# Summing the first chunks' softmax weights by a column of ones behind the values, in an attention that feeds a gated product of matrices

## The chip, the cores and the metric

The kernel runs on one core of one Trainium2 chip. The metric is device time in microseconds. Three timed runs of the kernel before gave 703.55, 704.68 and 706.06 us; the median is 704.68. Besides there is one profiled execution, whose trace all the durations come from.

## What is computed

An attention over 4 batches, 8 heads, 768 positions and 64 features gives rows x (3072 tokens of 512 features), and these go through three weight matrices. Cut to what matters:

```python
k_sum = k.reshape(B, H, nb, 32, D).max(axis=3)
v_sum = v.reshape(B, H, nb, 32, D).mean(axis=3)
scores_l = scale * q @ k.T                     # kept where |i - j| < 16
scores_s = scale * (q @ k_sum.T) + log(32)
a = exp(concat(scores_l, scores_s) - max)
a = a / (sum(a) + 1e-9)
x = a @ concat(v, v_sum)
out = (x @ w_a) * (x @ w_b) @ w_out            # 512 to 1536, and back to 512
```

Each query thus sees the keys less than 16 positions away and 24 summaries of blocks of 32 positions: the largest of the keys, the mean of the values. The weights come as 64-bit floats.

## The kernel before

**Chunks and items.** The 3072 tokens are 12 chunks u of 256 tokens, each of two groups t of 128. The 1536 columns between the matrices are 12 slices f. One item is a chunk and a slice: the *up* makes x times the slice of w_a and of w_b, 24 matmuls at L932; ACT copies one product (L949), DVE multiplies by the other (L952), ACT rounds (L954), DVE makes the rest (L957); the *down* at L968 multiplies by the slice of w_out, four matmuls with the rounded part (gh) and two with the rest (gl). PE needs 2.75 us for an up at full clock and about 1.37 for a down. x and the weights are each split into a high and a low part, and three of the four products are made. Chunk 0's first two slices come first, then chunk 1 and chunk 0 in turn, then chunk after chunk.

**Weights.** The 36 parts (a, b, o of slice 0, then of slice 1, and so on) come in 18 pairs. A pair's two halves are converted from the raw 64-bit words: ACT scales the high words into bank c0 (L289), DVE makes three steps (L297, L304, L310), ACT rounds to the high part (L342), POOL subtracts and adds (L347, L353) to get the low one.

**First attention (chunks 0 and 1, four groups).** A group's queries are turned by PE (L374) and copied to qT by ACT (L806). PE puts the mask into two PSUM banks (L571), adds the dots with kT (L583), DVE takes the maxima (L616), ACT makes the exponentials (L628), and each of these is followed by a read of the sum that it gathered, which goes back into the bank. DVE adds 1e-9 and takes the reciprocal (L637, L643) and spreads it on a diagonal (L650); PE multiplies s by this diagonal, which turns it and normalises it (L671); ACT copies (L683); PE multiplies with the values (L712), which gives x with features on the partitions; ACT makes its high part (L720), DVE its low (L723). Groups 0 and 2 use banks o0 and o1, s and pt; groups 1 and 3 use o2 and o3 and space lent by weights that come later.

**Keys and means.** Six key tiles are turned by PE; ACT copies a tile's first part into kT (L433), DVE takes the blocks' largest (L443), ACT copies its other part (L435); when all six are done, POOL writes the summaries behind the keys (L409). Six pieces of v are summed by matmuls with a matrix of 1/32 (L825, two for each piece, one for each of the two rows that lie side by side on a partition); ACT copies the means behind the values (L837), POOL copies them for the other group (L843).

**Third chunk (u = 2).** It is done by DVE transposes instead: DVE adds the mask (L608) and takes maxima, ACT makes exponentials, POOL multiplies by the reciprocal (L658), DVE turns s into pt by twelve transposes of 32 rows (L698), PE multiplies with the values into bank c0. Both its groups use pt and c0, so the second group's transposes stand behind the first group's values.

**What sets the order.** Every operation is put into a list with an engine, a rank, a time it is thought to take, and the names that it reads and writes. A planner (Work, ahead of the kernel) then walks a clock: each engine takes, of the operations whose inputs it thinks ready, the one with the lowest rank. CHAIN is 0, FIRST (chunk 0) 1, CONVERT 2, NEXT (chunk 1) 2.3, SOON (third chunk) 5. The engines then run their queues strictly in that order, and SP issues the transfers in its own.

Of the kernel before, what the change touches and what calls it, by code (L numbers as in the profile page):

```python
# [9 lines left out]
F32 = mybir.dt.float32  # L10
# [4 lines left out]
AF = mybir.ActivationFunctionType  # L15
# [69 lines left out]
def attention_moe(  # L85
# [23 lines left out]
    NU = NR * B  # L109
    G = CH // P  # L110
    CV = 512
    NW = 3 * NF // 2
    AHEAD = (7, 9, 17)
# [81 lines left out]
    for j in (*range(8, 13), *range(NW - 3, NW)):  # L195
        spaces[f"W{j}"] = wp.tile([P, 2048], F32, tag=f"W{j}", name=f"space{j}")

    kins = [kin, spaces["S1"][:, 2 * CV : 2 * CV + S + 32]]
# [30 lines left out]
    CHAIN, FIRST, CONVERT, NEXT, SOON, PREP, LATER = 0, 1, 2, 2.3, 5, 5.5, 6  # L229
# [34 lines left out]
    slots = [("S0", 0), ("S0", 2), ("S1", 2)]  # L264

    def convert(j):
        rank = CONVERT + j / 4
# [58 lines left out]
        for hs in spans:  # L326
# [13 lines left out]
            act(  # L340
                rank - 0.5, 0.25 + 0.37 * len(hs), f + rk, hi,
                lambda ms=ms, f8=f8: nc.scalar.copy(out=parted(0)[:, ms], in_=f8),  # L342
            )
# [73 lines left out]
    def first_keys():  # L417
        n = P // BLK
        for i in range(S // P):
# [7 lines left out]
            pe(FIRST, 0.85, [key], [bk], lambda bk=bk, x=x: turn(bank[bk], x))  # L427
            c0 = PER * i

            def put(lo, bk=bk, c0=c0):  # L430
                tr = bank[bk].rearrange("p (c x) -> p c x", x=P)
                if lo:
                    nc.scalar.copy(out=kT[:, :, c0 + 16 : c0 + WIN], in_=tr[:, :, : WIN - 16])  # L433
                else:
                    nc.scalar.copy(  # L435
                        out=kT[:, :, c0 + P : c0 + PER + 16], in_=tr[:, :, WIN - 16 :]
                    )
# [11 lines left out]
        for c in range(NP):  # L449
            work.add("-", 0, 0, 0, [f"ksi{i}" for i in range(6)], [f"ks{c}"], lambda: None)  # L450
            reads = [f"kT{x}{i}" for i in range(6) for x in "lh"]
            work.add("-", 0, 0, 0, reads, [f"kT{c}k"], lambda: None)
# [94 lines left out]
    def load_values(b, t, vw, keys, rank):  # L547
# [3 lines left out]
        for i, (e, r0, lo, hi) in enumerate((  # L551
# [5 lines left out]
                rank, 2.1 * (hi - lo), 215, (), [keys[i]], vw[e][r0 : r0 + hi - lo],  # L557
# [3 lines left out]
    def scores(u, t, qT, qk, s, sk, banks, diag=None, lead=None):  # L561
        kind = 0 if t == 0 else 2 if t == S // P - 1 else 1
        rank = rank_of(u) + (0.2 * (t % G) if u < FILL else 0)
        m, mk = nml[t % 2], f"nml{t % 2}"


        masked = u < FILL

        def masks():
            for h in range(2):  # L570
# [476 lines left out]
```

## Time and profile before

| | us |
|---|---|
| median of three runs | 704.68 |
| profiled execution | 704.12 |
| its span | 702.4 |
| PE busy | 682.8 |
| first up begins | 37.08 |
| third chunk's first two ups begin | 160.90 |

The span is the time from the first to the last instruction in the trace; the execution's own time is 1.7 us longer. Mean granted clock of PE: 0.998. Rows of a timeline give the start, the time, the engine, the line, the operation with its output and input, the count, and in brackets the time without work before it with the engine and line that ended it. SPq is the queue that issues transfers; there the time is that of issuing.

### The profile page before, as it was taken

Reading aid. Unit: us, or ns where it says so; the run is one execution under the profiler, and the core shown is the slowest. Engines: PE = TensorE matmul, PEld = TensorE weight load, DVE = VectorE, ACT = ScalarE, POOL = GpSimd, SP = SyncE. Lnnn points to the kernel's source line nnn. Section 1 sums busy time; section 2 is a strip of 40 time slices with the busy share of each in tenths; the row PEclk is TensorE's granted clock in tenths of the full one; section 3 lists DMA queues with packets and bytes.
Section 4 is the critical chain, followed back from the end, with each engine's and each line's share of the span. In section 5 each row is a group of like instructions: output and inputs, shape, how many; then the busy total and the mean of one; then the engine's idle time right before and its main releaser. Section 6 shows DMA issues by size and latency. Waiting matters only on the chain.

```text
span 702.4 us, 15093 instructions
## 1 busy us (share of the span) xinstructions
PE 682.8 (97%) x6000; PEld 626.4 (89%) x6000; DVE 436.4 (62%) x988; ACT 252.4 (36%) x795; POOL 181.3 (26%) x219
## 2 busy tenths in 40 slices
PE   6888999999999999999999999999999999999997
PEld 3778999988999999999999999999999999999996
DVE  2898999797767777666763776762762662311221
ACT  2976574533333314332332323332331431211211
POOL 4378976852433521130110101110110110000000
PEclk9999999999999999999999999999999999999999
DMA  9979773076233335220300330310310100000000
GB/s 229 265 173 309 267 168 126 6 152 145 64 89 96 83 79 107 50 56 19 82 8 17 69 68 2 87 25 1 83 24 1 54 21 1 31 1 1 31 1 31
DMA packets 154943, 54.84 MB, mean 78 GB/s; under 512 B 132456, under 2 KB 147816, under 8 KB 154872
## 3 DMA queue, kind: packets, MB, share of 16 engines
q1 hardware_dynamic: 154872, 53.88, 31.5%
q8 instruction: 47, 0.77, 0.5%
q14 instruction: 24, 0.20, 0.1%
HBM read 47.12 MB, written 6.29 MB: 76 GB/s over the span
## 4 chain that ended last, share of the span: by engine, by line
PE 79%; DVE 7%; POOL 7%; issue 3%; ACT 2%; DMA 2%; SPq 0%; POOLq 0%; ACTq 0%; DVEq 0%
PE h L932 48%; PE o L968 24%; POOL w L353 3%; POOL S L347 2%; DVE c L304 2%; PE o L712 1%; PE c L712 1%; PE o L583 1%; PE c L583 1%; DVE space L297 1%; POOL space L347 1%; DVE space L310 1%; DMA raw<-in_moe_w_b_dram 1%; ACT s L628 1%; DVE ksum L443 1%
## 5 line engine op out<-in xcount | busy, mean ns | idle before, releaser
L932 PEld LDWEIGHTS h<-x,w 128*128 128x128 f32 x3456 | 416.0, 189 | 14.0 <-DVE x L723 2.2
L932 PE MATMUL h<-x,w 128*128 128x256 f32 x3456 | 419.4, 278 | 1.9 <-DVE x L723 1.7
L952 DVE TENSOR_TENSOR h<-h,g 128x256 f32<-128x256 f32 x144 | 62.2, 432 | 164.9 <-ACT g L949 163.2
L968 PE MATMUL o<-w,gh 128*128 128x512 f32 x576 | 157.8, 396 | 1.3 <-ACT gh L954 1.2
L949 ACT COPY g<-h 128x256 f32<-128x256 f32 x144 | 53.8, 374 | 280.8 <-PE h L932 279.9
L968 PEld LDWEIGHTS o<-w,gh 128*128 128x128 f32 x576 | 98.8, 188 | 18.6 <-ACT gh L954 2.3
L698 DVE STREAM_TRANSPOSE pt<-s 32x256 f32<-32x256 f32 x240 | 104.6, 436 | 8.7 <-POOL s L658 4.5
L658 POOL TENSOR_TENSOR s<-s,nml 128x512 f32<-128x512 f32 x40 | 41.6, 1042 | 257.0 <-DVE nml L643 255.5
L968 PE MATMUL o<-w,gl 128*128 128x512 f32 x288 | 90.1, 394 | 0.0
L957 DVE TENSOR_TENSOR gl<-h,gh 128x256 fp32r<-128x256 f32 x144 | 60.7, 422 | 31.6 <-ACT gh L954 30.2
L628 ACT ACTIVATE s<-s,nml 128x128 f32<-128x128 f32 x160 | 62.7, 398 | 43.3 <-DVE nml L616 43.3
L954 ACT CAST gh<-h 128x256 fp32r<-128x256 f32 x144 | 53.6, 372 | 67.6 <-DVE h L952 67.3
L968 PEld LDWEIGHTS o<-w,gl 128*128 128x128 f32 x288 | 53.8, 188 | 11.9 <-issue 0.3
L513 POOL TENSOR_TENSOR S<-S 96x512 f32<-96x512 f32 (+3 forms) x48 | 33.6, 699 | 39.1 <-DMA S<-in_v_dram 30.7
L347 POOL TENSOR_TENSOR space<-space,w 128x1024 f32<-128x1024 f32 (+1 forms) x13 | 26.7, 2056 | 18.8 <-ACT w L342 13.9
L628 ACT ACTIVATION_READ_ACCUMULATOR s<-s,nml 128x1 f32 x160 | 31.1, 194 | 0.0
L289 ACT ACTIVATE c<-raw 128x512 f32<-128x512 f32 x36 | 23.2, 644 | 13.2 <-DVE S L297 5.1
L353 POOL TENSOR_TENSOR w<-space 128x1024 fp32r<-128x1024 f32 (+1 forms) x13 | 26.8, 2059 | 0.9
L637 DVE TENSOR_SCALAR nml<-nml 128x4 f32<-128x4 f32 x40 | 9.8, 244 | 26.9 <-ACT s L628 26.9
L616 DVE TENSOR_REDUCE nml<-s 128x4 f32<-128x512 f32 x40 | 25.4, 669 | 0.0
L409 POOL COPY kT<-ksum 128x144 f32<-128x144 f32 x16 | 4.7, 308 | 61.5 <-DVE ksum L491 54.7
L347 POOL TENSOR_TENSOR S<-S,w 128x512 f32<-128x512 f32 (+1 forms) x11 | 17.6, 1598 | 9.7 <-ACT w L342 9.6
(100 smaller groups left out, 454.2 us busy)
## 6 DMA issues: line engine op xcount, KB each, us to landing
raw<-in_moe_w_a_dram SPq DMA_DIRECT2D x12, 512.0 KB
raw<-in_moe_w_b_dram SPq DMA_DIRECT2D x12, 512.0 KB
raw<-in_moe_w_out_dram SPq DMA_DIRECT2D x12, 512.0 KB
out_dram<-S SPq DMA_DIRECT2D x24, 256.0 KB
qin<-in_q_dram SPq DMA_DIRECT2D x160, 32.0 KB
S<-in_v_dram SPq DMA_DIRECT2D x24, 192.0 KB
vw<-in_v_dram SPq DMA_DIRECT2D x18, 192.0 KB
kin<-in_k_dram SPq DMA_DIRECT2D x24, 100.0 KB
```

Of the source, the lines that this page charges most:

```text
L347: lambda ms=ms, f8=f8: nc.gpsimd.tensor_tensor(out=f8, in0=f8, in1=parted(0)[:, ms].bitcast(F32), op=ALU.subtract),
L353: lambda ms=ms, f8=f8, p8=p8: nc.gpsimd.tensor_tensor(out=parted(1)[:, ms], in0=f8, in1=p8, op=ALU.add),
L513: lambda: nc.gpsimd.tensor_tensor(out=out, in0=i0, in1=i1, op=ALU.add),
L628: lambda h=h, c=c, sums=sums: nc.scalar.activation(s[h][:, c, :], x[h][:, c, :], AF.Exp, bias=m[:, 0, h, c : c + 1], scale=1.0, accum_out= ...
L658: lambda h=h, r=r: nc.gpsimd.tensor_tensor(out=s[h], in0=s[h], in1=r[:, :, None].broadcast_to([P, NP, P]), op=ALU.mult,),
L698: lambda js=js, qs=qs: nc.vector.transpose(out=pv[js, :, qs], in_=sv[qs, :, js]),
L932: nc.tensor.matmul(ps, w[:, c, part, :], x[xpart][:, c, :], start=(i == 0), stop=(i == n - 1))
L949: act(CHAIN, 0.38, [hk], [gk], lambda: nc.scalar.copy(out=g, in_=pa))
L952: lambda: nc.vector.tensor_tensor(out=pa, in0=pb, in1=g, op=ALU.mult),
L954: act(CHAIN, 0.41, [hk], [ghk], lambda: nc.scalar.copy(out=gh, in_=pa))
L957: lambda: nc.vector.tensor_tensor(out=gl, in0=pa, in1=gh.bitcast(F32), op=ALU.subtract),
L968: nc.tensor.matmul(bank[ok[j]], (gh if first else gl)[:, js], w[:, :, part, :], start=(f == 0 and first and part == 0), stop=(f == NF - 1 ...
```

## The change

- **Sums by ones.** In the first attention the exponentials no longer gather sums. The values get a 65th column of ones (VP = 80 columns are set aside for a head), in W13 for groups 0 and 2 and in W12 and S1 for 1 and 3. s is turned as it is, by plain transposes. The values' matmul has the queries on the partitions and writes 65 columns for each of the eight heads, four heads in a bank; the 65th is the sum. Per bank DVE then adds 1e-9, takes the reciprocal and multiplies 256 columns; PE turns the 512 columns back (the function turn), and the split into high and low part follows.
- **Keys.** Both ACT copies of a key tile are one step, and DVE's reduction waits for it. The masks wait for the first key turn only.
- **POOL.** For the first four pairs the rounding to the high part goes from ACT to POOL. POOL adds the two rows of each v piece, and the matmuls for the means fall from twelve to six. POOL makes four copies of the means instead of two, and fills the ones.
- **Third chunk.** The second group's transposes get a place of their own (pown, in S0, cleared by POOL) and follow its scores; its values go to bank c1. The third chunk's loads of queries wait for the fifth pair's conversion.
- **Ranks.** NEXT goes from 2.3 to 1.5, the conversions' rank from 2 + j/4 to 2 + j/6, the loads of the first pair from 8 and 9 to 5 and 5.5; three slots that the conversions use in turn are renumbered.

The diff, cut to its core:

```diff
-    CHAIN, FIRST, CONVERT, NEXT, SOON, PREP, LATER = 0, 1, 2, 2.3, 5, 5.5, 6
+    CHAIN, FIRST, CONVERT, NEXT, SOON, PREP, LATER = 0, 1, 2, 1.5, 5, 5.5, 6
...
-            act(
-                rank - 0.5, 0.25 + 0.37 * len(hs), f + rk, hi,
-                lambda ms=ms, f8=f8: nc.scalar.copy(out=parted(0)[:, ms], in_=f8),
-            )
+            if j < FIRSTS:
+                pool(
+                    rank - 0.5, 0.1 + 0.55 * len(hs), f + rk, hi,
+                    lambda ms=ms, f8=f8: nc.gpsimd.tensor_copy(out=parted(0)[:, ms], in_=f8),
+                )
+            else:
+                act(
...
-            act(FIRST, 0.43, [bk], [f"kTl{i}"], lambda put=put: put(True))
-            act(FIRST, 0.33, [bk], [f"kTh{i}"], lambda put=put: put(False))
+            act(FIRST, 0.75, [bk], [f"kT{i}"], put)
             dve(
-                FIRST, 0.6, [bk], [f"ksi{i}"],
+                FIRST, 0.6, [bk, f"kT{i}"], [f"ksi{i}"],
...
+    def early_scores(u, t, qT, qk, s, sk, banks):
...
+                act(
+                    rank, 0.26, [f"{mk}m{h}", banks[h]], [sk[h]],
+                    lambda h=h, c=c: nc.scalar.activation(
+                        s[h][:, c, :], x[h][:, c, :], AF.Exp, bias=m[:, 0, h, c : c + 1]
+                    ),
+                )
+
+    def early_values(u, t, s, sk, banks, pt, vw, vk):
...
+        def turned(h):
+            for c in range(NP):
+                nc.tensor.transpose(bank[banks[h]][:, c * P : (c + 1) * P], s[h][:, c, :], ident)
...
+        def weigh(j):
+            for i in range(NP):
+                g = NP * j + i
+                for e in range(2):
+                    es = slice(e * QT, (e + 1) * QT)
+                    nc.tensor.matmul(
+                        ps[j][es, i, : D + 1], d[:, g % 2, g // 2, es], vw[e][:, g, : D + 1],
+                        start=True, stop=True, tile_position=(0, e * QT),
+                    )
...
+        for j in range(2):
+            l = m[:, 1, j, :]
+            dve(
+                rank, 0.15, [banks[j]], [f"{mk}l"],
+                lambda j=j, l=l: nc.vector.tensor_scalar(
+                    out=l, in0=ps[j][:, :, D], scalar1=1e-9, scalar2=None, op0=ALU.add
+                ),
+            )
+            dve(rank, 0.15, [], [f"{mk}l"], lambda l=l: nc.vector.reciprocal(out=l, in_=l))
+            dve(
+                rank, 0.4, [banks[j], f"{mk}l"], [sk[0]],
+                lambda j=j, l=l: nc.vector.tensor_tensor(
+                    out=xn[:, j * 256 : (j + 1) * 256].rearrange("p (g d) -> p g d", d=D),
+                    in0=ps[j][:, :, :D], in1=l[:, :, None].broadcast_to([P, NP, D]), op=ALU.mult,
+                ),
+            )
+        pe(-1, 0.6, [sk[0]], [banks[1]], lambda: turn(bank[banks[1]], xn))
+        split(u, t, banks[1])
...
+        for x in vw0 + vw1:
+            nc.gpsimd.memset(x[:, :, D : D + 1], 1.0)
...
         for n in range(6):
-            pe(FIRST + 0.5, 1.0, [vin[n][1], mk], ["h0"], lambda n=n: means(n))
+            x, key = vin[n]
+            pool(
+                FIRST, 0.7, [], [key],
+                lambda x=x: nc.gpsimd.tensor_tensor(
+                    out=x[:, :, :D], in0=x[:, :, :D], in1=x[:, :, D:], op=ALU.add
+                ),
+            )
+            pe(FIRST + 0.5, 0.5, [key, mk], ["h0"], lambda n=n: means(n))
...
-            qk += blocks(98, f"qin.{c}", qin[:, c, :], q, b, c, r * CH)
+            qk += blocks(
+                98, f"qin.{c}", qin[:, c, :], q, b, c, r * CH, ["done4"] if u == FILL else ()
+            )
...
             begin(1)
+            pool(rank, 0.9, (), ["S0.2", "S0.3"], lambda: nc.gpsimd.memset(pown, 0.0))
+            transposes(u, True)
             yield
             values(*end(0))
             bring(1)
-            turned(1)
             values(*end(1))
```

**ACT in the first two groups.** This is ACT's queue before, from the second group's copy on (h_75 is the bank of v's means, vw_165 and vw_166 the values' places, raw_259 the second weight pair).

```order
L683 COPY space_188<-o_73 128x512
L342 CAST w_417<-space_195 128x4x128
L837 COPY vw_165<-h_75 32x512
L289 ACTIVATE c_77<-raw_259 128x512
L837 COPY vw_166<-h_75 32x512
L683 COPY space_188<-o_74 128x512
```

And this is it in the changed kernel, where L685 is the exponential, L703 the copy of turned s, L897 the copy of the means, L292 the scaling of weights and raw_268 the second pair.

```order
L703 COPY pt<-o_72 128x512
L685 ACTIVATE space_191<-o_74,nml_185 128x128
L685 ACTIVATE space_191<-o_73,nml_185 128x128
L685 ACTIVATE space_191<-o_74,nml_185 128x128
L897 COPY space_193<-h_75 32x8x64 x2
L685 ACTIVATE space_191<-o_73,nml_185 128x128
L685 ACTIVATE space_191<-o_74,nml_185 128x128
L685 ACTIVATE space_191<-o_73,nml_185 128x128
L685 ACTIVATE space_191<-o_74,nml_185 128x128
L703 COPY space_188<-o_73 128x512
L292 ACTIVATE c_77<-raw_268 128x512
L703 COPY space_188<-o_74 128x512
```

The means' copies have moved from behind the second group's exponentials into the middle of them; the second pair's scaling has stayed between the two copies of that group's turned s.

**DVE at the same place.** Before, behind the last of the four maxima (L616), with the additions, reciprocals and diagonals of the first group's two banks (o_71, o_72) and conversion steps (L297, L310):

```order
L616 TENSOR_REDUCE nml_185<-o_74 128x4
L637 TENSOR_SCALAR o_71<-o_71 128x4
L643 RECIPROCAL o_71<-o_71 128x4
L650 TENSOR_TENSOR pt<-ident,o_71 128x512
L297 TENSOR_SCALAR space_195<-c_77 128x512
L637 TENSOR_SCALAR o_72<-o_72 128x4
L643 RECIPROCAL o_72<-o_72 128x4
L650 TENSOR_TENSOR pt<-ident,o_72 128x512
L310 SCALAR_TENSOR_TENSOR space_195<-raw_213,c_78 128x512
```

Changed kernel, behind the last of the four maxima (L677): the addition, the reciprocal and the multiplication of the first group (L729, L733, L736), then the second pair's first step (L300).

```order
L677 TENSOR_REDUCE nml_185<-o_74 128x4
L729 TENSOR_SCALAR nml_184<-o_71 128x4
L733 RECIPROCAL nml_184<-nml_184 128x4
L736 TENSOR_TENSOR s<-o_71,nml_184 128x256
L729 TENSOR_SCALAR nml_184<-o_72 128x4
L733 RECIPROCAL nml_184<-nml_184 128x4
L736 TENSOR_TENSOR s<-o_72,nml_184 128x256
L300 TENSOR_SCALAR space_195<-c_77 128x512
```

The addition and the reciprocal have stayed in this place, but they read what the values' matmul leaves and no longer what the exponentials leave, and the conversion steps now stand behind both banks.

**SP's loads.** Before (raw_213 is the first weight pair, space_189 the keys' and queries' place):

```order
L225 DMA space_189<-in_k_dram 128x8x64 x2
L225 DMA space_189<-in_q_dram 128x8x64 x2
L254 DMA raw_213<-in_moe_w_a_dram 128x4x256
L254 DMA raw_213<-in_moe_w_b_dram 128x4x256
L225 DMA space_190<-in_v_dram 128x4x128 x4
```

In the changed kernel, down to the first of the three loads of the second group's values (space_192; the other two follow):

```order
L257 DMA raw_215<-in_moe_w_a_dram 128x4x256
L257 DMA raw_215<-in_moe_w_b_dram 128x4x256
L228 DMA space_189<-in_q_dram 128x8x64 x2
L228 DMA space_190<-in_v_dram 128x4x128 x4
L228 DMA space_191<-in_v_dram 128x4x128 x2
L228 DMA space_193<-in_v_dram 80x8x64
L228 DMA space_193<-in_v_dram 32x8x64
L228 DMA space_193<-in_v_dram 64x8x64
L228 DMA space_188<-in_q_dram 128x8x64 x2
L257 DMA raw_268<-in_moe_w_out_dram 128x1024
L257 DMA raw_268<-in_moe_w_a_dram 128x4x256
L228 DMA space_192<-in_v_dram 96x8x64
```

The first weight pair has moved ahead of the queries; the rows of v for the second group follow raw_268 as they followed raw_259 before.

**PE ahead of the third chunk.** Before, the last values of that chunk (L712, pt and c_77) stand in the middle of the last down:

```order
L968 MATMUL o_74<-w_1633,gh_176 128x512 x2
L712 MATMUL c_77<-pt,vw_165 64x64 x2
L712 MATMUL c_77<-pt,vw_166 64x64 x2
L712 MATMUL c_77<-pt,vw_165 64x64 x2
L712 MATMUL c_77<-pt,vw_166 64x64 x2
L712 MATMUL c_77<-pt,vw_165 64x64 x2
L712 MATMUL c_77<-pt,vw_166 64x64 x2
L712 MATMUL c_77<-pt,vw_165 64x64 x2
L712 MATMUL c_77<-pt,vw_166 64x64 x2
L968 MATMUL o_73<-w_1633,gl_178 128x512
L968 MATMUL o_74<-w_1633,gl_178 128x512
L932 MATMUL h_75<-x_0_169,w_417 128x256
```

In the changed kernel they read their own place (S_186), go to the other bank (c_78), and have two downs behind them (L1028):

```order
L765 MATMUL c_78<-S_186,vw_165 64x64 x2
L765 MATMUL c_78<-S_186,vw_166 64x64 x2
L1028 MATMUL o_73<-w_1494,gh_175 128x512 x2
L1028 MATMUL o_74<-w_1494,gh_175 128x512 x2
L1028 MATMUL o_73<-w_1494,gl_177 128x512
L1028 MATMUL o_74<-w_1494,gl_177 128x512
L1028 MATMUL o_73<-w_1571,gh_176 128x512 x2
L1028 MATMUL o_74<-w_1571,gh_176 128x512 x2
L1028 MATMUL o_73<-w_1571,gl_178 128x512
L1028 MATMUL o_74<-w_1571,gl_178 128x512
L992 MATMUL h_75<-x_0_169,w_333 128x256
```

The values have moved one down earlier, so that more of PE's work lies between them and the up that needs their result.

More of the change, by code (lines that the diff above doesn't have):

```diff
@@ L109, in attention_moe @@
     NU = NR * B
+    VP = 80
     G = CH // P
@@ new lines, in dots @@
+    def dots(t, qT, banks, alone):
+        for c in range(NP):
+            for h in range(2):
+                hs = slice(h * D, (h + 1) * D)
+                for e in range(2):
+                    es = slice(e * QT, (e + 1) * QT)
+                    c0 = PER * t + QT * e
+                    nc.tensor.matmul(
+                        bank[banks[h]][es, c * P : (c + 1) * P], qT[hs, c, es],
+                        kT[hs, c, c0 : c0 + P],
+                        start=alone, stop=alone or c == NP - 1, tile_position=(h * D, e * QT),
+                    )
@@ new lines, in transposes @@
+    def transposes(u, own=False):
+        rank = rank_of(u)
+        sv = sbuf.rearrange("p h c x -> p (h c) x")
+        dst, key = (pown, "pu") if own else (pbuf, "pt")
+        pv = dst.rearrange("p h c x -> p (h c) x")
+        for i, kb in enumerate(((0, 1, 3), (1, 2, 3), (0, 1, 2), (1, 2, 3))):
+            qs = slice(32 * i, 32 * (i + 1))
+            for j in kb:
+                js = slice(32 * j, 32 * (j + 1))
+                dve(
+                    rank, 0.45, SK + ["S0.2"] * own, [f"{key}{i}{j}"],
+                    lambda js=js, qs=qs: nc.vector.transpose(out=pv[js, :, qs], in_=sv[qs, :, js]),
+                )
@@ new lines, in early_scores @@
+    def early_scores(u, t, qT, qk, s, sk, banks):
+        kind = 0 if t == 0 else 1
+        rank = rank_of(u) + 0.2 * (t % G)
+        m, mk = nml[t % 2], f"nml{t % 2}"
+        x = [bank[n].rearrange("p (c x) -> p c x", x=P) for n in banks]
+        for h in range(2):
+            pe(
+                rank + 0.1, 0.9, ["first"], [banks[h]],
+                lambda h=h: nc.tensor.matmul(
+                    x[h], ident, mask[:, kind, None, :].broadcast_to([P, NP, P]),
+                    start=True, stop=False,
+                ),
+            )
+        pe(-1, 1.2, [*qk] + KT, banks, lambda: dots(t, qT, banks, False))
+        for h in range(2):
+            dve(
+                rank, 0.6, [banks[h]], [f"{mk}m{h}"],
@@ L916, in attention @@
                 bring(i)
-                turned(i)
+                transposes(u)
                 lead.append(products(*end(i)))
         if u == NU - 1:
-            reads, bk, fn, split = lead.pop()
+            reads, bk, fn, then = lead.pop()
             pe(-1, 1.1, reads, [bk], fn)
-            split()
+            then()
         yield
```

306 lines of the change are left out of this document (135 added, 171 removed).

## The prediction

> **What bounds the kernel now.** I read the page first, for the shares and the cost of single operations.
>
> ```profile
> span 702.4 us, 15093 instructions
> ...
> PE 682.8 (97%) x6000; PEld 626.4 (89%) x6000; DVE 436.4 (62%) x988; ACT 252.4 (36%) x795; POOL 181.3 (26%) x219
> ...
> L952 DVE TENSOR_TENSOR h<-h,g 128x256 f32<-128x256 f32 x144 | 62.2, 432 | 164.9 <-ACT g L949 163.2
> ...
> L698 DVE STREAM_TRANSPOSE pt<-s 32x256 f32<-32x256 f32 x240 | 104.6, 436 | 8.7 <-POOL s L658 4.5
> ```
>
> PE is busy 97% of the span, so only its 20 us without work and whatever matmul work falls away can be won. Where those 20 us lie, the busy times by stretch tell (columns: window, its length, busy time of PE, PEld, DVE, ACT, POOL, PE clock, DMA share, GB/s).
>
> ```profile
> 0.00:10.00 10.00, 5.53 (x15) 3.36 (x16) 1.37 (x3) 1.71 (x2) 7.67 (x51) 1.00 0.90 179
> 10.00:20.00 10.00, 6.79 (x86) 4.51 (x88) 4.97 (x8) 5.64 (x15) 1.50 (x8) 1.00 1.14 294
> 20.00:30.00 10.00, 9.49 (x70) 8.00 (x63) 9.14 (x21) 8.94 (x38) 0.28 (x1) 1.00 1.04 226
> 30.00:37.08 7.08, 6.38 (x113) 4.67 (x112) 6.13 (x10) 7.03 (x14) 6.80 (x7) 1.00 1.12 324
> 37.08:65.74 28.66, 25.41 (x244) 22.41 (x240) 25.65 (x49) 19.73 (x56) 21.68 (x14) 0.94 0.87 221
> 47.24:50.64 3.40, 3.40 (x19) 3.40 (x18) 3.26 (x8) 2.41 (x9) 2.79 (x4) 0.50 1.06 339
> 65.74:167.00 101.26, 98.09 (x791) 89.71 (x791) 93.16 (x194) 49.84 (x120) 74.68 (x53) 1.00 0.58 156
> 167.00:702.40 535.40, 531.14 (x4703) 493.73 (x4701) 296.01 (x707) 159.50 (x554) 68.66 (x91) 1.00 0.19 44
> ```
>
> Behind 167 us PE works 99% of the time, and the change touches nothing there. All is decided ahead of it: by when the first up starts (37.08), when the first up of the second chunk is over (65.74), and the 3.17 us without work from there to 167. The PE timeline names the events (start, time, line, operation; in brackets the wait before and who ended it).
>
> ```profile
> 18.32 1.10 PE L583 MATMUL o<-kT,qT 64*64 64x128 f32 x32 [1.40 <-POOL kT L409]
> ...
> 29.19 0.60 PE L374 MATMUL o<-ident,space 128*128 128x128 f32 x4
> ...
> 31.28 1.20 PE L712 MATMUL h<-pt,vw 128*64 128x64 f32 x32
> ...
> 37.08 3.00 PE L932 MATMUL h<-x,w 128*128 128x256 f32 x24
> ...
> 46.03 1.13 PE L671 MATMUL o<-pt,s 128*128 128x128 f32 x8 [2.02 <-ACT space L628]
> 46.91 4.61 PE L932 MATMUL h<-x,w 128*128 128x256 f32 x24
> ...
> 60.12 5.62 PE L932 MATMUL h<-x,w 128*128 128x256 f32 x47 [0.31 <-DVE x L723]
> 66.38 1.20 PE L968 MATMUL o<-w,gh 128*128 128x512 f32 x4 [0.63 <-ACT gh L954]
> ...
> 156.20 1.21 PE L968 MATMUL o<-w,gh 128*128 128x512 f32 x4 [0.61 <-ACT gh L954]
> ...
> 160.90 5.80 PE L932 MATMUL h<-x,w 128*128 128x256 f32 x47 [1.34 <-DVE x L723]
> ```
>
> **The sum's base.** The profiled execution took 704.12 us, 1.7 more than its span; the median of the three runs is 704.68. Differences are worked out against the profiled one and taken off the median.
>
> **Keys and first scores.** Keys, queries and exps follow one another on ACT and POOL:
>
> ```profile
> 10.32 0.32 ACT L435 COPY kT<-c 128x192 f32<-128x192 f32 x1 [0.76 <-DVE ksum L443]
> ...
> 20.79 0.37 ACT L628 ACTIVATE s<-o,nml 128x128 f32<-128x128 f32 x1 [0.66 <-DVE nml L616]
> 21.05 0.16 ACT L628 ACTIVATION_READ_ACCUMULATOR s<-o,nml 128x1 f32 x1
> ...
> 29.01 0.62 ACT L342 CAST w<-space 128x512 fp32r<-128x512 f32 x1
> 29.66 0.58 ACT L837 COPY vw<-h 32x512 f32<-32x512 f32 x1
> ```
>
> ```profile
> 17.38 1.05 POOL L409 COPY kT<-ksum 128x144 f32<-128x144 f32 x4 [6.80 <-DVE ksum L443]
> 29.72 1.28 POOL L347 TENSOR_TENSOR space<-space,w 128x512 f32<-128x512 f32 x1 [11.28 <-ACT w L342]
> 31.06 1.27 POOL L843 COPY space<-vw 32x512 f32<-32x512 f32 x2
> ```
>
> Before, each key tile alternates ACT, DVE, ACT, and ACT stands 0.76 us per tile for DVE's reduction. With both copies ahead of the reduction those six waits go (4.5 us), so the key summaries are in about 3 to 4 us earlier and stop deciding: 18.4 becomes 14 to 15. Then the queries decide, since the first pair's a and b now load ahead of them. Queries of both groups end at 1.57 (keys) + 1.05 + 0.52 = 3.15 MB; the windows give 1.79 MB by 10 us and 294 GB/s behind it, so 14.6 us, plus 1 us that I allow for landing. First dots end near 16.9 and the exps begin near 18.1, 2.7 us earlier than 20.79. Without the 0.16 us read behind each, they also take less.
>
> **Values of the first group.** What held the values at 31.28 was the copy of v's sums at 29.66, queued on ACT behind the exps of two groups and a rounding of 0.62. In the new order it stands in the middle of the second group's exps. The last v piece ends at 4.72 MB, 20.0 us; with landing, POOL's addition (about 0.7, scaled from L347's 1.28 for twice the elements) and three matmuls, the copy runs near 22.6 and the values near 23.7, 7.6 us earlier.
>
> **The second group eats most of that.** Its values need rows of v that load as SP's 14th to 16th entries, behind both halves of raw_268: 4.72 + 0.36 + 0.52 + 1.05 + 0.39 = 7.05 MB. The windows give 6.99 MB by 30 us, so 30.2, landing 31.2. ACT also stands at raw_268's first half (6.13 MB, 27.2 us) ahead of this group's second copy, but that is over by then. Behind the values comes the new loop: per bank an addition, a reciprocal and a multiplication by 256 columns on DVE, then a turn on PE.
>
> ```profile
> 22.64 0.17 DVE L637 TENSOR_SCALAR o<-o 128x4 f32<-128x4 f32 x1
> 22.84 0.19 DVE L643 RECIPROCAL o<-o 128x4 f32<-128x4 f32 x1
> ```
>
> With the multiplication at L952's 0.43, one bank costs 0.79 and two 1.6; the turn is 0.6 (row at 29.19), four hand-offs some 0.4: 2.6 us in series. 31.3 + 1.2 (values) + 2.6 + hi and lo of 0.6 and 0.7 gives 36.4; where DVE or ACT is inside a conversion step, up to 1.5 more. So the first up starts at 36.4 to 37.9, −0.7 to +0.8: the large gain of the first group is hidden behind a transfer.
>
> **To the second chunk.** Here the PE work shrinks. A group's s was turned by matmuls with the diagonal (eight records in 1.13 us for a bank, so 2.0 for two); plain transposes cost 0.6 a bank as in the row at 29.19, and the added turn another 0.5: 0.5 less per group, 1.0 for the third and fourth. From 37.08 to 65.74 PE was busy 25.41, of which 1.86 came from an up at half clock (4.61 instead of 2.75). That leaves 23.55 − 1.0 = 22.5 at full clock. Start 37.2 + 22.5 = 59.7. To this come waits: the loop of the fourth group, 2.6 us, in which PE has only two downs and pieces of turns (38% busy by my walk, so 1.6 open), and 0.3 to 1.4 at the third's exps. End 61.6 to 63.0 instead of 65.74; I take a gain of 3.4, ends 2.7 and 4.1.
>
> From this comes the clock. Before, PE stood 2.02 us, had been about 40% busy over 3.4 us, and the granted clock was 0.50 for the next 3.40 us. The new order has a similar stretch around the fourth group. I put the chance of such a stretch at two thirds, so 1.2 us of 1.86; net 2.2.
>
> The Trainium skill ("TensorE: Matmul & The Clock Gate", Part 1: The HAM clock gate) gives half rate as what follows at least one idle window of about 3.4 us; by that rule no stretch would be slow, since the gaps I expect are under 2.7 us, and the total would be 1.2 lower. The trace disagrees: 2.02 us sufficed.
>
> **Conversions.** POOL takes four pairs' roundings from ACT. The nearest POOL row is the copy of 32 partitions, 0.64 each; ACT needed 0.62. Eight halves give 5.1 us, the six additions 4.2, four copies 2.5 (two were there), the clearing of 128x1024 about 1: 11.5 added. Cover is POOL's 11.28 us wait before 29.72. If the roundings cost as much as a two-input operation (1.28), 5 us more fall on POOL, which then finishes the fourth pair at about its old time and gains nothing; below 0.6 I see no reason.
>
> The Trainium skill ("GPSIMD Engine Reference", 4.1 Engine selection) advises VectorE rather than GpSimd for elementwise work, two inputs being about twice as slow there and one input near line rate. The one-input part agrees with 0.64 beside 0.62; the two-input part speaks against the additions, which by it cost 2 us more than on DVE, beside other work.
>
> Weights arrive sooner for another reason, too:
>
> ```profile
> 30.50 12.73 SPq L225 DMA_DIRECT2D qin<-in_q_dram  x16
> ```
>
> These sixteen small loads held SP for 12.73 us ahead of the later weights. Now they wait for the fifth pair's conversion and come behind eight more halves.
>
> **Late waits.** Of the 3.17 us without work from 65.74 to 167, the 0.63 at 66.38 stays, since the same up, up, down order stands there. The 1.34 at 160.90 waits for the third chunk's second lo: its twelve transposes (12 x 0.436 = 5.2 us of DVE) had to follow the first group's values, which read the same place. With a place and a bank of its own they follow its scores at once, and I get lo 1.1 us before it is needed. Two downs (2.75 us) instead of 0.46 us of one now stand between the values and the next up. The 0.61 at 156.20 goes with it. About 1.0 stays, so 2.1 is gained; ends 0.5 (another chain takes over) and 2.5.
>
> **Sum.** 2.2 + 2.1 = 4.3: profiled 699.8, median 704.68 − 4.3 = 700.4; with the ends 698.0 to 702.5.
>
> **The rivals.** A measurement of this kernel can tell about 0.3%, 2.1 us.
>
> *The whole lead is kept* (0.10). No half clock, group two's v rows ahead of my estimate, and the first up at 35: 4.1 + 2.5 + 2 = 8.6, up to 9.5, so 695 to 697. For it: the window 30 to 37 moved 324 GB/s. Against: SP's order.
>
> *Nothing to be seen* (0.20). The front gives only 2.7, a full half-clock stretch takes 1.86 of it, and the late waits stay as they were because the keys' preparation for the next chunk on DVE replaces the one removed. 704.68 − 0.8 = 703.9. For it: DVE is busy 93.16 of 101.26 us there.
>
> *Slower through the serial loop* (0.18). DVE takes its queue in order: the addition of the first group waits for the values from about 19.8 to 24.4, with all conversion steps behind it; before, DVE was busy 9.14 of 10 us there. If the same happens in groups three and four, each exposes its 2.6 us, the halves behind it come as much later, and a second half-clock stretch follows: 5.2 + 1.86 = 7.1, less 2.1 late and about 2.2 from the exps and the lighter turns: +2.8, 707.5. It decides from where the second chunk's first up ends later than 67.8 (65.74 + 2.1). Against: in this order the third group has an up and the dots to cover it.
>
> **How the numbers follow.** The forecast has 0.52, and with the whole lead kept faster is 0.62; same 0.20; slower 0.18. The likeliest case alone spans 698.0 to 702.5. The range of 695.0 to 705.5 takes in the larger gain and the case of no change, and leaves out nearly only the slower rival.
>
> **What would show it.** Right: first dots near 16; first group's values near 24 and the second's near 31, waiting for a DMA; first up at 36.4 to 37.9; second chunk's first up over by 61.6 to 65 (with the slow stretch); no wait of 1 us around 155 to 165; POOL's rounding near 0.64. Wrong: a first up under 35 or over 39, the rounding at over 1 us, two stretches at clock 0.50, or a new wait of PE for w between 65 and 140.

## The result, and the profile after

The changed kernel took 695.66 us (median of four runs, 694.84 to 697.38) beside 704.14 us for the kernel before in the same session. The ratio is 0.9876, with a 95% interval of 0.9858 to 0.9895: 8.7 us faster, where 4.3 had been forecast. The direction was right; the gain was twice the forecast.

The profiled execution took 697.38 us, with a span of 695.6, and was the slowest of the four. All durations below are its own, so they explain 6.8 us (702.4 − 695.6); where the rest may come from stands at the end. First the busy times by stretch, with columns as in the prediction, the borders moved to the places that answer to the old ones.

```profile
10.00:20.00 10.00, 7.79 (x87) 5.66 (x86) 7.40 (x13) 4.82 (x12) 5.46 (x18) 0.83 1.21 289
20.00:30.00 10.00, 8.07 (x70) 5.89 (x69) 4.56 (x11) 8.72 (x24) 9.36 (x12) 1.00 1.22 245
...
36.20:64.00 27.80, 24.05 (x233) 21.23 (x234) 25.13 (x52) 17.28 (x40) 21.67 (x12) 0.94 0.99 246
46.81:52.20 5.39, 5.39 (x55) 5.27 (x56) 3.60 (x10) 1.93 (x6) 5.09 (x3) 0.71 0.95 267
64.00:161.00 97.00, 96.84 (x793) 89.58 (x792) 89.16 (x188) 49.31 (x119) 72.06 (x48) 1.00 0.58 153
```

The clocks of 0.83 and 0.71 come from two stretches of 3.41 us in which the granted clock was 0.50; the kernel before had one (47.24 to 50.64).

```profile
15.76:19.17 3.41, 3.41 (x52) 3.08 (x56) 1.73 (x3) 0.64 (x2) 2.59 (x4) 0.50 1.21 292
46.48:49.89 3.41, 3.08 (x35) 2.99 (x36) 2.28 (x8) 1.61 (x6) 3.25 (x3) 0.50 0.93 230
```

From 64 to 161 us PE is now without work for 0.16 us, where the old kernel had 3.17 between 65.74 and 167. Next PE's timeline.

```profile
24.44 0.33 PE L718 MATMUL o<-space,pt 128*64 128x65 f32 x2 [0.77 <-ACT space L897]
...
31.73 0.24 PE L718 MATMUL o<-S,space 128*64 128x65 f32 x1 [1.05 <-DMA S<-in_v_dram]
...
36.20 0.38 PE L992 MATMUL h<-x,w 128*128 128x256 f32 x1 [0.24 <-ACT x L749]
37.50 2.90 PE L992 MATMUL h<-x,w 128*128 128x256 f32 x23 [0.92 <-DVE x L752]
...
46.12 0.30 PE L718 MATMUL o<-space,pt 128*64 128x65 f32 x2 [2.09 <-DMA space<-in_v_dram]
46.81 1.97 PE L718 MATMUL o<-space,pt 128*64 128x65 f32 x30 [0.39 <-DMA space<-in_v_dram]
48.70 3.55 PE L992 MATMUL h<-x,w 128*128 128x256 f32 x24
...
58.47 5.61 PE L992 MATMUL h<-x,w 128*128 128x256 f32 x48
...
154.76 5.63 PE L992 MATMUL h<-x,w 128*128 128x256 f32 x48
```

The first group's values start at 24.44 (31.28 before), the second's wait for their rows of v until 31.73, and the first up starts at 36.20 with one matmul and goes on at 37.50 (37.08 before). The second chunk's first up is over at 58.47 + 5.61 = 64.08 (65.74 before), and the third chunk's first two at 154.76 + 5.63 = 160.39 (160.90 + 5.80 = 166.70 before). So the 6.8 us come in three parts: 1.66 by the second chunk, 4.65 from there to the third chunk (100.96 us became 96.31, with the same matmuls), and 0.5 behind it (535.70 became 535.21). Of the 4.65 only some 3.0 are time that the view shows as without work (3.17 became 0.16).

ACT, DVE and POOL in the front show the steps: the exponentials without reads, the first group's sums, the rounding.

```profile
19.40 2.26 ACT L685 ACTIVATE s<-o,nml 128x128 f32<-128x128 f32 x8 [2.04 <-DVE nml L677]
```

```profile
25.84 0.16 DVE L729 TENSOR_SCALAR nml<-o 128x4 f32<-128x4 f32 x1 [4.67 <-PE o L718]
26.03 0.18 DVE L733 RECIPROCAL nml<-nml 128x4 f32<-128x4 f32 x1
26.25 0.42 DVE L736 TENSOR_TENSOR s<-o,nml 128x256 f32<-128x256 f32 x1
```

```profile
16.58 0.73 POOL L888 TENSOR_TENSOR space<-space 128x256 f32<-128x256 f32 x1 [2.65 <-DMA space<-in_v_dram]
17.26 0.61 POOL L346 CAST w<-space 128x512 fp32r<-128x512 f32 x1
```

### The profile page after: what moved, and what is told of

Read it like the earlier page. It is cut to its first block, busy times and chain, and to the rows that moved or that the text cites. A ratio compares the mean times of both kernels' runs of the same rounds, so it can differ in the third digit from the quotient of the medians.

```text
span 695.6 us, 15044 instructions
## 1 busy us (share of the span) xinstructions
PE 677.5 (97%) x5972; PEld 622.7 (90%) x5972; DVE 432.1 (62%) x988; ACT 245.4 (35%) x757; POOL 192.3 (28%) x239
## 4 chain that ended last, share of the span: by engine, by line
PE 91%; DMA 3%; SPq 2%; DVE 2%; issue 0%; ACT 0%; ACTq 0%
PE h L992 55%; PE o L1028 28%; PE o L633 2%; PE c L765 2%; PE c L633 2%; PE o L765 1%; SPq L228 1%; DMA raw<-in_moe_w_a_dram 1%; SPq L257 1%; DMA space<-in_q_dram 1%; DMA S<-in_v_dram 1%; DVE S L653 1%; PE o L668 0%; DVE c L307 0%; DVE space L313 0%
## 5 line engine op out<-in xcount | busy, mean ns | idle before, releaser
L1028 PE MATMUL o<-w,gh 128*128 128x512 f32 x576 | 157.9, 396 | 0.1
L1028 PEld LDWEIGHTS o<-w,gh 128*128 128x128 f32 x576 | 99.0, 188 | 17.9 <-issue 1.5
L653 DVE STREAM_TRANSPOSE pt<-s 32x256 f32<-32x256 f32 x228 | 99.3, 436 | 7.6 <-POOL s L620 3.4
L1028 PE MATMUL o<-w,gl 128*128 128x512 f32 x288 | 89.9, 394 | 0.0
L605 ACT ACTIVATE s<-s,nml 128x128 f32<-128x128 f32 x160 | 62.7, 396 | 47.4 <-DVE nml L596 47.4
L1028 PEld LDWEIGHTS o<-w,gl 128*128 128x128 f32 x288 | 53.9, 188 | 11.8 <-DVE gl L1017 0.2
L292 ACT ACTIVATE c<-raw 128x512 f32<-128x512 f32 x36 | 23.2, 644 | 16.0 <-DVE space L300 8.9
L613 DVE TENSOR_SCALAR nml<-nml 128x4 f32<-128x4 f32 x40 | 7.5, 188 | 30.2 <-ACT s L605 30.2
L362 POOL TENSOR_TENSOR w<-S 128x512 fp32r<-128x512 f32 (+1 forms) x11 | 17.6, 1599 | 0.9
```

What stands on the lines that cost most here:

```text
L362: lambda ms=ms, f8=f8, p8=p8: nc.gpsimd.tensor_tensor(out=parted(1)[:, ms], in0=f8, in1=p8, op=ALU.add),
L605: lambda h=h, c=c: nc.scalar.activation(s0[h][:, c, :], s0[h][:, c, :], AF.Exp, bias=m[:, 0, h, c : c + 1], scale=1.0, accum_out=m[:, 1, h ...
L653: lambda js=js, qs=qs: nc.vector.transpose(out=pv[js, :, qs], in_=sv[qs, :, js]),
L1028: nc.tensor.matmul(bank[ok[j]], (gh if first else gl)[:, js], w[:, :, part, :], start=(f == 0 and first and part == 0), stop=(f == NF - 1 ...
```

## Experiments

Each kernel was timed in five rounds beside the kernel before on the same chip. The ratio is to that kernel, and its interval is in brackets; the changed kernel's own is 0.9876 (0.9858 to 0.9895). A gain in us is the ratio's, on 704.

### The late waits: a place of its own, or the order of the conversions

Two parts of the change could have taken away the waits between 65 and 167 us: the third chunk's own place and bank, and the conversions' rank. First the place, alone and undone.

```diff
-                    rank, 0.45, sk, [f"pt{i}{j}"],
+                    rank, 0.45, sk + ["S0.2"] * own, [f"{key}{i}{j}"],
...
+            pool(rank, 0.9, (), ["S0.2", "S0.3"], lambda: nc.gpsimd.memset(pown, 0.0))
+            turned(1)
             yield
             values(*end(0))
             bring(1)
-            turned(1)
```

> The kernel before with the third chunk's part of the change alone: own place and own bank for its second group, transposes right behind its scores, the slots renumbered. Theory A (most of what I missed lies in the third chunk: a wait that the timeline shows as 1.34 costs PE more, counted from start to start): 3 to 3.6 us faster than before, about 701. Rival B (what I missed lies in the first attention and the weights): 1.3 to 2 us faster at most, 702.5 or more.

Measured: 0.9943 (0.9926 to 0.9959), 4.0 us faster. Theory A is borne out by this run. The converse takes the place out of the changed kernel (and with it the second group's own bank):

```diff
-            if u == FILL and i:
-                return u, t0 + i, "c1", (pown, PU + ["S0.2", "S0.3"])
...
-            pool(rank, 0.9, (), ["S0.2", "S0.3"], lambda: nc.gpsimd.memset(pown, 0.0))
-            transposes(u, True)
             yield
             values(*end(0))
             bring(1)
+            transposes(u)
```

> The changed kernel without the third chunk's part: its second group shares place and bank again, its transposes stand behind the first group's values. Theory A: 3 to 3.6 us slower than the changed kernel, about 699, with a wait of PE for the second group's lo ahead of the third chunk's first up. Rival B: at most 2 us slower, 697.5.

Measured: 0.9877 (0.9858 to 0.9896), no different from the changed kernel. Theory A falls: the place helps the old kernel, but in the changed one it does nothing that can be measured. Something else removes the waits there. The rank was tried next, one number alone and undone.

```diff
-        rank = CONVERT + j / 4
+        rank = CONVERT + j / 6
```

> The kernel before with one number changed: the conversions' rank 2 + j/6 in place of 2 + j/4, so that the last conversions (j from 12) go ahead of the third chunk's operations on DVE, ACT and POOL. Theory E (this rank removes the late waits, since conversions no longer stand among the third chunk's steps): 3 to 4 us faster than before, the waits from 118 to 161 us gone. Theory F (the late waits go because the front starts the conversions earlier): within 1 us of before.

> The changed kernel with the conversions' rank back at 2 + j/4. Theory E: 3 to 4 us slower than the changed kernel if the third chunk's own place does not cover it, 1 to 2 if it does. Theory F: within 1 us of the changed kernel.

Measured: the number alone gives 0.9942 (0.9921 to 0.9964), 4.1 us faster; taken back in the changed kernel it gives 0.9941 (0.9917 to 0.9964), 4.6 us slower than the changed kernel. Theory E is nearer in both, though with the number alone one late wait is left (0.93 us at 152.94), where none was expected; F falls as an account of the whole. How it works is seen in the busy times of the two kernels with the old front. Before:

```profile
100.00:120.00 20.00, 20.00 (x147) 18.78 (x146) 19.48 (x39) 9.99 (x26) 14.07 (x8) 1.00 0.56 160
120.00:140.00 20.00, 19.79 (x166) 18.12 (x166) 16.17 (x30) 10.41 (x23) 15.83 (x13) 1.00 0.02 5
```

With the rank at j/6 alone:

```profile
100.00:120.00 20.00, 20.00 (x149) 18.90 (x148) 18.91 (x37) 13.98 (x39) 18.94 (x12) 1.00 0.52 146
120.00:140.00 20.00, 20.00 (x190) 18.12 (x190) 17.63 (x37) 8.31 (x24) 15.67 (x14) 1.00 0.24 51
```

Before, from 100 to 120 us DVE is full (19.48), twelve transposes of the third chunk among its work (109.84 to 116.66), and POOL is left with 14.07. Its longest wait ends at 122.06, with a rounding by ACT that itself had to wait for DVE's L310:

```profile
122.06 1.30 POOL L347 TENSOR_TENSOR S<-S,w 128x512 f32<-128x512 f32 x1 [6.04 <-ACT w L342]
```

From 120 to 140 DVE has only 16.17, since it now waits for POOL's low parts. DVE's timeline of the kernel before at the end of its conversions:

```profile
136.27 0.69 DVE L297 TENSOR_SCALAR S<-c 128x512 int32<-128x512 int32 x1 [0.69 <-POOL w L353]
...
138.13 0.68 DVE L310 SCALAR_TENSOR_TENSOR S<-raw,c 128x512 f32<-128x512 uint32 x1
```

And that of the kernel with the rank alone:

```profile
127.12 0.69 DVE L310 SCALAR_TENSOR_TENSOR S<-raw,c 128x512 f32<-128x512 uint32 x1
...
129.29 1.78 DVE L698 STREAM_TRANSPOSE pt<-s 32x256 f32<-32x256 f32 x4
```

The last conversion step ends at 127.8 instead of 138.8, and the third chunk's transposes follow it. POOL gets its work while DVE goes on (18.94 of 20), and DVE hardly waits for it. Both parts together on the kernel before tell whether they are one gain or two.

> The kernel before with both the conversions' rank at 2 + j/6 and the third chunk's own place. If these are two ways to the same gain: 4 to 5 us faster than before, about 699.5. If they remove different waits: 7 to 8 us, about 696.5.

Measured: 0.9935 (0.9917 to 0.9954), 4.6 us: one gain that either can bring, not two. With the old rank the place also has a price. In the changed kernel with j/4 no late wait over 0.4 us is left ahead of the third chunk, but PE's timeline shows a new one at 197 us, for the next chunk's sums of v; of the 4.6 us that this kernel loses, 2.2 lie behind 161 us:

```profile
197.28 0.34 PE L765 MATMUL c<-pt,vw 128*64 128x64 f32 x4 [0.70 <-DMA vw<-S]
198.02 1.03 PE L765 MATMUL c<-pt,vw 128*64 128x64 f32 x28 [0.41 <-DMA vw<-S]
```

### The front by itself

The changed kernel without both (rank j/4, no own place) keeps the first attention, its loads, the keys and POOL's work.

```diff
-        rank = CONVERT + j / 6
+        rank = CONVERT + j / 4
...
-            transposes(u, True)
             yield
             values(*end(0))
             bring(1)
+            transposes(u)
...
```

> The changed kernel with both things undone that each removed the late waits: the conversions' rank is 2 + j/4 again and the third chunk's second group has no place of its own. What stays is the first attention's change with its loads, keys, POOL work and the second chunk's rank. Theory G (front and late waits add up): 4 us faster than before, about 699.7, with the late waits back. Rival H (the front alone is worth what the profiled execution shows at the second chunk's first up, 1.7): about 702.

Measured: 0.9929 (0.9912 to 0.9946), 5.0 us faster than before. Theory G is nearer: 5.0 and the rank's 4.1 make 9.1, the whole is 8.7. Part of the front's 5.0 is gained late: of the waits between 65 and 161 us 1.71 are left (0.18, 0.36, 0.40 and 0.77) beside 3.14 before.

The kept profiles tell the parts apart. Each row is one execution, in us: when the second chunk's first up is over, how long PE then takes until the third chunk's first two ups are over (22 ups and their downs in every row), and what is left behind that.

| front | rank | own place | first part | until the third chunk | behind |
|---|---|---|---|---|---|
| before | j/4 | no | 65.7 | 101.0 | 535.7 |
| before | j/4 | yes | 65.6 | 97.5 | 535.2 |
| before | j/6 | no | 64.5 | 96.8 | 536.1 |
| before | j/6 | yes | 65.5 | 96.8 | 535.9 |
| changed | j/4 | no | 61.5 | 99.6 | 535.2 |
| changed | j/4 | yes | 63.6 | 97.6 | 537.4 |
| changed | j/6 | no | 61.9 | 96.1 | 535.5 |
| changed | j/6 | yes | 64.1 | 96.3 | 535.2 |

Until the third chunk the changed front takes off 1.4 us by itself; behind that front the number takes off 3.5, the place 2.0, and both no more than the number alone.

In the first part the four kernels with the changed front have the same operations in the same order on every engine up to 90 us, and still they differ by 2.6 us. In the profile of the kernel without both parts PE waits less for the third group's rows of v (0.28 and 0.84 us, beside 2.09 and 0.39 in the changed kernel's), and no stretch at half clock follows:

```profile
44.35 0.30 PE L718 MATMUL o<-space,pt 128*64 128x65 f32 x2 [0.28 <-DMA space<-in_v_dram]
45.49 1.12 PE L718 MATMUL o<-space,pt 128*64 128x65 f32 x30 [0.84 <-DMA space<-in_v_dram]
46.53 2.99 PE L989 MATMUL h<-x,w 128*128 128x256 f32 x24
```

It is the same with the other two: 0.64 and 0.65 without a slow stretch (61.9), 1.33 and 0.65 with one (63.6). The changed kernel's own profile thus shows the front at its slowest.

Which of the front's orders matters was tried by undoing one at a time in the changed kernel: the third chunk's query loads allowed early again, the first weight pair behind the queries again, the second chunk's rank at 2.3 again.

```diff
-                98, f"qin.{c}", qin[:, c, :], q, b, c, r * CH, ["done4"] if u == FILL else ()
+                98, f"qin.{c}", qin[:, c, :], q, b, c, r * CH, ()
```

```diff
-    for i, rank in enumerate((5, 5.5, 17, 17.5, 19, 20)):
+    for i, rank in enumerate((8, 9, 17, 17.5, 19, 20)):
```

```diff
-    CHAIN, FIRST, CONVERT, NEXT, SOON, PREP, LATER = 0, 1, 2, 1.5, 5, 5.5, 6
+    CHAIN, FIRST, CONVERT, NEXT, SOON, PREP, LATER = 0, 1, 2, 2.3, 5, 5.5, 6
```

> The changed kernel with the third chunk's sixteen small query loads allowed early again: SP issues them ahead of later weights and of the rows of v for groups three and four. The prediction gave these loads 12.7 us of SP. If that is worth something: PE waits longer for the third group's rows and for weights, 1.5 to 3 us slower than the changed kernel. If the transfers are covered: within 0.7 us.

> The changed kernel with the first weight pair loaded behind the queries, as before. The exponentials then start about 3 us earlier and the first conversions 2 to 3 us later. By the prediction's reading (the second group's rows of v set the first up): within 0.7 us. If the conversions' lead carries the front's gain: 1.5 to 3 us slower.

> The changed kernel with the second chunk's rank back at 2.3, so that conversions go ahead of more of its steps and an up stands ahead of two downs. By the prediction nothing hangs on this rank: within 0.7 us. Rival: the second chunk comes later, 1 to 2 us slower.

Measured: 0.9939 (0.9918 to 0.9959), 4.4 us slower than the changed kernel; 0.9925 (0.9906 to 0.9944), 3.4 us slower; 0.9882 (0.9861 to 0.9902), no difference. The first two cost more than the expectations had, and for the weight pair the prediction's reading (within 0.7) missed: in that profile the first up starts at 39.61, with no wait for the second group's rows of v. The two orders of loads carry most of the front's gain, and they hang together (4.4 and 3.4 are more than the 5.0 that there is to lose). With the query loads early, SP issues them from 33.90 on, and the third group's rows of v only at 47.60; PE's timeline:

```profile
50.48 0.33 PE L718 MATMUL o<-space,pt 128*64 128x65 f32 x2 [1.81 <-DMA space<-in_v_dram]
52.75 1.97 PE L718 MATMUL o<-space,pt 128*64 128x65 f32 x30 [1.95 <-DMA space<-in_v_dram]
```

### POOL's rounding, and the keys

```diff
+            if j < 4:
+                pool(
+                    rank - 0.5, 0.1 + 0.55 * len(hs), f + rk, hi,
+                    lambda ms=ms, f8=f8: nc.gpsimd.tensor_copy(out=parted(0)[:, ms], in_=f8),
+                )
+            else:
...
```

> The kernel before with only the rounding of the first four pairs moved from ACT to POOL. Theory A (ACT was not what bound the front, POOL's idle time hides the work): within 1 us of before. Rival C (ACT bound the front): 1.5 to 2.5 us faster. Rival D (POOL is late with the low parts of the fourth pair): 1 to 2 us slower.

> The changed kernel with the rounding of the first four pairs back on ACT. Theory A: within 1 us of the changed kernel. Rival C: 1.5 to 2.5 us slower. Rival D: up to 1 us faster.

Measured: alone on the kernel before 1.0024 (1.0008 to 1.0041), 1.7 us slower, in size what rival D has; but PE's long waits there are for DVE (2.40 us at 46.54, 2.22 at 58.70), each with 3.41 us at half clock behind or around it, so how it comes about stays open. Back on ACT in the changed kernel (FIRSTS = 0) 0.9879 (0.9859 to 0.9899), no difference. The rounding is covered there, and no more.

The keys alone, both ACT copies ahead of the reduction in the kernel before:

```diff
-            act(FIRST, 0.43, [bk], [f"kTl{i}"], lambda put=put: put(True))
-            act(FIRST, 0.33, [bk], [f"kTh{i}"], lambda put=put: put(False))
+            act(FIRST, 0.75, [bk], [f"kTl{i}", f"kTh{i}"], lambda put=put: (put(True), put(False)))
...
-                FIRST, 0.6, [bk], [f"ksi{i}"],
+                FIRST, 0.6, [bk, f"kTl{i}"], [f"ksi{i}"],
```

> The kernel before with only the key tiles' two ACT copies ahead of DVE's reduction. The prediction's step: the six waits of 0.76 go, the dots start 3 to 4 us earlier than 18.3 and so do the exponentials. Since the first group's values wait for the means of v, and the second's for a transfer, I expect nothing measurable of it in the total, within 1 us of before; a rival that has the front's start decide would have 2 to 3 us.

Measured: 1.0024 (1.0007 to 1.0042), 1.7 us slower where within 1 had been expected, though the dots start at 14.79 instead of 18.32 and the first up at 35.63 instead of 37.08. What follows is a longer wait of PE for the third group's rows of v (3.55 us at 53.36), and half clock from 52.90 to 59.73:

```profile
52.70:54.40 1.70, 0.57 (x6) 0.42 (x8) 1.51 (x4) 1.55 (x4) 1.69 (x1) 0.56 0.76 144
54.40:56.10 1.70, 1.70 (x32) 1.70 (x32) 0.67 (x1) 0.00 (x0) 1.63 (x1) 0.50 1.00 262
56.10:57.80 1.70, 1.70 (x32) 1.54 (x28) 1.08 (x2) 0.76 (x2) 0.73 (x1) 0.50 1.04 383
57.80:59.50 1.70, 1.70 (x10) 1.30 (x7) 1.34 (x3) 1.70 (x3) 0.00 (x0) 0.50 1.07 367
```

A gain ahead of a transfer that doesn't come sooner is idle time of PE, and here that idle time was also paid for in clock.

### Loads for the second and third group, and the clock

The prediction held the rows of v behind raw_268 responsible for the first up. Here they go ahead of it:

```diff
-        load_values(0, 1, vw1, vk1[:3], 18)
+        load_values(0, 1, vw1, vk1[:3], 16.7)
```

> The changed kernel with the rows of v for the second group loaded ahead of the second weight pair instead of behind it. If the second group's values wait for that transfer alone, as the prediction has it: their matmuls start 3 to 4 us earlier than 31.7 and the first up some 2 to 3 us earlier than 36.2 to 37.5; the total falls by 1 to 3 us unless the second weight pair, now 1.5 us later, holds the second up. Rival: the first up stays, since ACT and DVE set it.

Measured: the first up starts at 33.88, 2.3 us earlier, so the transfer did set it in the changed kernel. But the whole is 0.9916 (0.9895 to 0.9938), 2.8 us slower than the changed kernel: the second weight pair is late, PE stands 3.59 us at 44.7 for an L300 step of DVE, and the clock is at half for 6.8 us behind it.

The next kernel loads the third chunk's first rows of v behind the fifth pair's conversion.

```diff
-            load_values(b, t0 + i, vbuf, VK[:3], 97)
+            load_values(
+                b, t0 + i, vbuf, VK[:3], 97, ["done4"] if u == FILL and i == 0 else ()
+            )
...
```

> The changed kernel with the third chunk's first rows of v loaded behind the fifth pair's conversion, like its queries. SP then has 4.1 us less ahead of the third group's rows of v, for which PE waits 2.09 and 0.39 us. Expected: that wait gone or under 0.5 us and 1.5 to 3 us faster than the changed kernel, about 693.5. Rival: the wait passes to the conversions or to DVE, within 0.7 us.

Measured: 0.9902 (0.9884 to 0.9919). The third group's wait is gone, but PE now waits 1.26 us for DVE's lo at 51.56 and 1.70 for ACT's gh at 60.78; nothing is won. The rival was nearer.

The last two add four matmuls whose results nobody reads, to keep PE busy where it waits (two ahead of the first queries' turn, two ahead of the third group's values), without and with this later load.

```diff
+        def warm(n):
+            for i in range(n):
+                nc.tensor.matmul(
+                    bank["h1"].rearrange("p (c x) -> p c x", x=P), ident,
+                    mask[:, 0, None, :].broadcast_to([P, NP, P]), start=True, stop=True,
+                )
...
```

> The changed kernel with four matmuls of the mask added whose results nobody reads: two ahead of the first queries' turn and two ahead of the third group's values, where PE waits. Nothing else moves in any queue. If the stretches at half clock come from PE's being idle there: no such stretch at 15 to 19 and at 46 to 50, the third group's values back at 1.1 us instead of 1.97 and the next up at 2.75 instead of 3.4; 1 to 2 us faster than the changed kernel, so about 694. The first stretch should give nothing, since a transfer decides behind it. If the clock does not follow PE's work, no change but the 0 to 0.5 us that the added matmuls may cost.

> Both of the former together. If each works by its own mechanism, 2 to 3.5 us faster than the changed kernel; if the later load already removes the idle time that slows the clock, no more than the later load alone.

Measured: 0.9904 (0.9882 to 0.9925) and 0.9914 (0.9896 to 0.9931), no gain; the second is 2.7 us slower than the changed kernel, clear of the intervals. In the first, both slow stretches are gone, but another one has come where there was none:

```profile
15.30:17.00 1.70, 1.22 (x8) 0.84 (x8) 1.67 (x3) 0.60 (x1) 0.00 (x0) 1.00 1.09 309
25.50:27.20 1.70, 1.43 (x30) 1.29 (x30) 0.28 (x2) 1.52 (x5) 1.59 (x2) 0.74 0.80 190
27.20:28.90 1.70, 1.70 (x14) 1.58 (x11) 1.25 (x5) 0.18 (x1) 1.61 (x2) 0.50 1.04 380
46.50:48.20 1.70, 1.42 (x10) 0.55 (x10) 1.70 (x4) 1.40 (x4) 1.70 (x2) 1.00 1.04 201
```

For the first stretch the clock does follow PE's work: it stands between 15 and 20 us in all nine kept profiles with the changed front's first loads and no added matmuls, and in neither of the two with them. For the second that is not shown, since it is missing in some profiles without added matmuls, too. And filling two pauses of one to two us did not keep another slow stretch from coming at 26 us. No kernel tried beats the changed one by more than the intervals.

## Why the prediction was half right

**Keys and exponentials:** right in kind, 19.40 for a forecast 18.1. **First group's values:** 24.44 for 23.7. **Second group:** right to 0.2 us; its values waited for the rows of v until 31.73 (31.3 forecast), the first up came at 36.20 and 37.50 (36.4 to 37.9), and vw1_early shows that the transfer decided.

**To the second chunk:** the gross term was 3.4 (2.7 to 4.1), less 1.2 for a slow stretch that was given two chances in three. The two profiles of this front without that stretch show 4.2 and 3.9 (61.5 and 61.9 beside 65.7), the two with it 2.1 and 1.7. So the term was right in kind, and 2.2 is near what an execution with the stretch gains; what one without it gains is up to 2 us more. In the changed kernel's profile the stretch (46.81 to 52.20, mean clock 0.71) costs 5.39 x 0.29 = 1.6. (The term's latest end is 62.7 by its own figures, 59.7 + 1.6 + 1.4, and not 63.0.)

**The clock:** two stretches at clock 0.50 were named as a sign of being wrong, and there are two. The first (from 15.76) was not foreseen; it lies ahead of the wait for the second group's rows, and in the kernel with added matmuls, which lacks it, the first up comes no sooner (37.87). The Trainium skill ("TensorE: Matmul & The Clock Gate", Part 1: The HAM clock gate) would have had no slow stretch, since no wait reached its idle window of about 3.4 us. This trace disagrees: 2.09 and 0.39 us of waiting were enough, as 2.02 had been before, while 0.28 and 0.84 were not.

**Conversions:** POOL's rounding at 0.61 and its addition at 0.73 were priced right, and act_rounds shows that it moves nothing. The loads that SP issues later were named there, but got no term of the sum; qin_free gives them 4.4 us. The front's 3.4 takes the new order as given, in which they are late already, so it may hold them without naming them.

**Late waits:** this is the step of the prediction that failed, by its size and by its cause. "About 1.0 stays, so 2.1 is gained; ends 0.5 (another chain takes over) and 2.5": measured, 4.65. In the profiled execution, 6.8 us faster for a forecast 4.3, this is the whole of what was missed (2.55 more here, 0.5 less in the front, 0.5 more behind). The size: I read the time without work (3.17) as all that could be won. PE's timeline of the kernel before shows it is not.

```profile
122.76 1.81 PE L932 MATMUL h<-x,w 128*128 128x256 f32 x14
124.78 1.41 PE L932 MATMUL h<-x,w 128*128 128x256 f32 x10 [0.21 <-POOL w L353]
...
159.17 0.39 PE L932 MATMUL h<-x,w 128*128 128x256 f32 x1
160.90 5.80 PE L932 MATMUL h<-x,w 128*128 128x256 f32 x47 [1.34 <-DVE x L723]
```

Twenty-four matmuls of an up take 2.75 us, so 14 take 1.60; from 122.76 to 124.78 it is 2.02, a loss of 0.42 where the bracket says 0.21. One matmul takes 0.11; from 159.17 to 160.90 it is 1.73, a loss of 1.62 where the bracket says 1.34. Measured from start to start these two waits cost 0.2 and 0.3 us more than their brackets. The premise that only the time without work (and lighter matmul work) can be won was too narrow.

The cause: I gave the gain to the third chunk's own place. In the changed kernel the place is not needed (no_third): 1.4 us come with the front and 3.5 with the conversions' rank, which the prediction passed over as a number. That more of PE's work should stand between the last values and the next up was right, but the number brings that, too: without the place the values stand at 149.28 and are followed by 1.95 us of downs ahead of the up, where it was 0.76 in the kernel before.

**The rivals:** the serial loop did not cost what the slower rival feared. DVE stood 4.67 us at 25.84 as forecast, once; later groups waited under 1 us. The rival with the whole lead kept came nearest in size (695 to 697), by a way that it did not describe: it had no half clock and the first up at 35. That the stated range takes in 695.66 rests on this rival, and so it is luck.

**Left open:** the four runs of the changed kernel differ by 2.5 us, and two of them are over 2 us faster than the profiled one. The profiles of the same front show what can make such a difference, a longer wait for the third group's rows of v with half clock behind it. For the runs without a profile this is not shown: the mean clocks of the four (0.995, 0.997, 0.996, 0.994 for 697.38, 694.84, 695.08, 696.25 us) don't order them. Why the rows come sooner in one execution than in another, and what part of the front is the lighter turning alone, was not found out.

## What to carry to other kernels

Count what a wait costs from start to start of the waiting engine's operations, not by the idle time in the view. In a schedule made by ranks, a changed rank is an edit of its own and must be walked on the engine that is full at that time: here one number, which let DVE finish the conversions before it turned the next chunk's s, was worth half of a change of several hundred lines. Two edits that each bring 4 us alone may be the same 4 us. And a single profile of a stretch that hangs on a transfer is one draw: here the same order of work took 2.6 us more in one execution than in another.

## What the runs showed of the hardware

Stretches at half clock came in 3.4 us or in about twice that, after waits of 1.7 to 3.6 us or several shorter ones; the two longest waits (3.55 and 3.59) were followed by 6.8 us. With the same order of work, waits of 1.1 and 1.3 us in two pieces had no such stretch behind them, and waits of 2.0 and 2.5 had one. The kernels that brought the first up forward but let PE stand later (keys_only, vw1_early) lost by it more than they had won.
